# Moving group 1's K and q transposes, one slot of its value products, a split weight cast and paired remainder scores in a fused attention + MLP kernel

## Chip, cores and metric

The kernel runs on one core of a Trainium2 chip. The metric is the device time of one execution in microseconds (us), of which the profile's span is about 1.7 us less.

## The reference, cut to what matters

```python
# q, k, v: (8 blocks, 8 heads, 576 tokens, 64); x: (4608, 512); w_in: (512, 2048); w_out: (2048, 512)
k_p = k.reshape(B, H, 72, 8, D).mean(axis=3)          # K and v pooled by 8 along the sequence
v_p = v.reshape(B, H, 72, 8, D).mean(axis=3)
attn = softmax(q @ k_p.T / sqrt(D))
x = concat_heads(attn @ v_p)
out = gelu_tanh(x @ w_in) @ w_out
```

## The kernel before

The 4608 tokens are worked off in nine groups: 512 tokens of each of the eight blocks, and one remainder group R with the last 64 tokens of every block. While TensorE runs the MLP of one group, the attention of the next is slipped between its matmuls. Python "hooks" say before which matmul (slot) a piece of work is put into TensorE's stream. In group 0, slots 0 to 127 are the hidden product (0.109 us each), 128 to 191 the output product (0.216 us each). Hooks set only the order on each engine; semaphores do the waiting.

Names in the views: kvb is pooled K or v, kbd and vbd are the block-diagonal weights made of them ("spread"), kT and qT are transposes, sc the scores, e their exponentials, r one over the sums of e, eb the softmax weights, eT their transpose, xo the value products, xT their cast, which is the input of the hidden product, gT the hidden product after gelu, osb an output before its store. w_out's "rows 6 and 7" are its blocks 6 and 7 of 128 rows.

```python
def cast_w_out(f0, f1, eng):                 # f32 staging buffer -> bf16 weights
    copy(eng, w_out_b[:, f0:f1, :], w_out_s[f0 // 8][:, f0 - o:f1 - o, :])

def norm(g, j, eng):                         # softmax: two SBUF inputs, e and r
    sums(g, j); nc.vector.reciprocal(out=r, in_=den)
    eng.tensor_tensor(out=o, in0=e, in1=r.to_broadcast(...), op=ALU.mult)

def spread_v(b, eng, parts=(0, 1, 2)):       # pooled v into block-diagonal weights vbd
    ...
# hooks of group 0's MLP, which carry group 1's attention
at(hooks, 72, pool, 1, 0, 4)                 # K pooled on VectorE, c = 4 after it
at(hooks, 80, cast_q, 1, 0, 2, nc.vector)
at(hooks, 108, k_transpose_pe, 1, 0, 5)
at(hooks, 108, k_spread, 1, [nc.vector, nc.vector])     # kT (PSUM) -> kbd
for j in range(4):
    at(hooks, [115, 119, 123, 126][j], q_transpose_pe, 1, j, nc.vector, "sc")
at(hooks, 110, cast_w_out, 0, 1, nc.gpsimd)  # then 1..2, 2..4, 4..6, 6..8 on GpSimd
...
for j in range(4):
    at(hooks, [128, 131, 142, 146][j], scores, 1, j)
    at(hooks, [128, 131, 142, 146][j], exps, 1, j)
    at(hooks, [142, 146, 150, 154][j], norm, 1, j, nc.vector)
    at(hooks, [142, 146, 150, 154][j], e_transpose_dma, 1, j)
for i in range(2):
    at(hooks, 160, pool, 1, 5 + 2 * i, 7 + 2 * i)        # v pooled
    at(hooks, 160, spread_v, 1, nc.gpsimd, (0, 1) if i == 0 else (2,))
tail_of_attention(hooks, 1, 187)             # value products, then xT on ScalarE
```

For later groups the K and q transposes are DMA transposes; R's scores are sixteen 64 x 64 matmuls per j.

The softmax here doesn't subtract the row's maximum and nothing guards it: scores larger than these inputs give would overflow.

## Time and profile before

| | before |
|---|---|
| median of the first three runs | 295.06 us (294.63 to 295.13) |
| span of the profiled run | 293.1 us |
| TensorE busy | 286.0 us, 98% |
| start of group 1's third hidden matmul | 52.78 us |
| end of GpSimd's last w_out cast | 39.87 us |

A line of the timeline has the start in us, the length in us, the engine, the line of the kernel, the operation, output and inputs, the count, and in brackets the idle time before it with what ended it.

### The profile page before, as it was taken

Reading aid. Unit: us, or ns where it says so; the run is one execution under the profiler, and the core shown is the slowest. Engines: PE = TensorE matmul, PEld = TensorE weight load, DVE = VectorE, ACT = ScalarE, POOL = GpSimd, SP = SyncE. Lnnn points to the kernel's source line nnn. Section 1 sums busy time; section 2 is a strip of 40 time slices with the busy share of each in tenths; the row PEclk is TensorE's granted clock in tenths of the full one; section 3 lists DMA queues with packets and bytes.
Section 4 is the critical chain, followed back from the end, with each engine's and each line's share of the span. In section 5 each row is a group of like instructions: output and inputs, shape, how many; then the busy total and the mean of one; then the engine's idle time right before and its main releaser. Section 6 shows DMA issues by size and latency. Waiting matters only on the chain.

```text
span 293.1 us, 4588 instructions
## 1 busy us (share of the span) xinstructions
PE 286.0 (98%) x1739; PEld 143.5 (49%) x1739; DVE 141.0 (48%) x235; ACT 156.5 (53%) x233; POOL 64.3 (22%) x86
## 2 busy tenths in 40 slices
PE   8889899999999999999999999999999999999996
PEld 4678754445444544454445444544444544444444
DVE  5891878176517460747075706580738100920012
ACT  1586484778076706671577256725673377436500
POOL 4575443221303040204002400240024000100000
PEclk9999999999999999999999999999999999999999
DMA  7999999996799369946994599159944900351012
GB/s 231 353 384 345 379 383 208 348 246 165 149 296 279 104 134 287 265 128 134 277 269 148 126 252 298 14 122 247 284 141 103 179 27 2 83 114 38 0 72 72
DMA packets 73301, 56.32 MB, mean 192 GB/s; under 512 B 45888, under 2 KB 55488, under 8 KB 73280
## 3 DMA queue, kind: packets, MB, share of 16 engines
q1 hardware_dynamic: 73136, 55.98, 70.3%
q8 instruction: 13, 0.21, 0.3%
q14 instruction: 8, 0.07, 0.1%
q10 hardware_dynamic: 144, 0.07, 0.1%
HBM read 36.70 MB, written 9.44 MB: 157 GB/s over the span
## 4 chain that ended last, share of the span: by engine, by line
PE 87%; DMA 8%; DVE 1%; SPq 1%; ACT 1%; POOL 0%; issue 0%
PE mm L360 41%; PE mm L344 38%; DMA kv<-in_k_dram 5%; DMA q_sb<-in_q_dram 3%; PE xo L310 3%; PE sc L214 2%; PE mm L388 1%; PE mm L355 1%; SPq L99 1%; ACT xT L79 1%; PE xo L319 1%; DVE kv L132 1%; PE tp L199 0%; POOL q_b L81 0%; PE sc L221 0%; DVE kv L133 0%
## 5 line engine op out<-in xcount | busy, mean ns | idle before, releaser
L360 PE MATMUL mm<-w_out_b,gT 128*128 128x512 bf16 x560 | 128.8, 379 | 0.0
L344 PE MATMUL mm<-xT,w_in_b 128*128 128x512 bf16 x512 | 112.0, 379 | 0.2 <-ACT xT L79 0.2
L346 ACT ACTIVATE gT<-mm 128x512 bf16<-128x512 f32 x128 | 76.4, 597 | 38.4 <-PE mm L344 38.4
L360 PEld LDWEIGHTS <-gT 128*128 128x128 bf16 x560 | 52.8, 98 | 59.7 <-issue 2.9
L344 PEld LDWEIGHTS <-w_in_b 128*128 128x128 bf16 x512 | 50.1, 98 | 60.8 <-issue 0.5
L81 DVE COPY osb<-mm 128x512 f32<-128x512 f32 (+2 forms) x37 | 24.3, 658 | 58.9 <-PE mm L360 52.7
L79 ACT CAST xT<-xo 128x1024 bf16<-128x1024 f32 (+1 forms) x18 | 16.6, 967 | 56.5 <-PE xo L310 48.2
L154 POOL TENSOR_TENSOR vbd<-kvb,vmask 128x256 bf16<-128x256 bf16 (+2 forms) x40 | 21.5, 559 | 104.5 <-DVE kvb L134 104.3
L236 DVE TENSOR_REDUCE den<-e 128x8 f32<-128x576 f32 x36 | 26.5, 736 | 36.9 <-ACT e L229 36.9
L132 DVE TENSOR_TENSOR kv<-kv 128x1024 f32<-128x1024 f32 (+3 forms) x19 | 21.7, 1144 | 38.0 <-DMA kv<-in_v_dram 31.8
L229 ACT ACTIVATE e<-sc 128x576 f32<-128x576 f32 x36 | 22.5, 650 | 9.5 <-ACT e L229 5.6
L248 DVE TENSOR_TENSOR eb<-e,r 128x576 bf16<-128x576 f32 x24 | 22.6, 943 | 1.0 <-DVE r L245 0.2
L81 POOL CAST q_b<-q_sb 128x2048 bf16<-128x2048 f32 (+2 forms) x9 | 17.4, 1937 | 14.2 <-DMA q_sb<-in_q_dram 14.2
L248 POOL TENSOR_TENSOR eb<-e,r 128x576 bf16<-128x576 f32 x6 | 6.9, 1150 | 58.3 <-ACT e L229 31.1
L355 PE MATMUL mm<-xT,w_in_b 128*128 128x256 bf16 x128 | 15.5, 273 | 0.5 <-DVE xT L81 0.5
L214 PE MATMUL sc<-kbd,qT 128*128 128x144 bf16 x128 | 13.3, 226 | 0.3 <-DVE qT L81 0.2
L214 PEld LDWEIGHTS <-qT 128*128 128x128 bf16 x128 | 10.0, 98 | 7.0 <-issue 0.5
L355 PEld LDWEIGHTS <-w_in_b 128*128 128x128 bf16 x128 | 12.1, 98 | 2.1 <-issue 0.6
L357 ACT ACTIVATE gT<-mm 128x512 bf16<-128x512 f32 x16 | 9.4, 597 | 6.5 <-PE mm L355 6.5
L133 DVE TENSOR_TENSOR kv<-kv 128x512 f32<-128x512 f32 (+3 forms) x19 | 12.4, 651 | 0.6
L557 ACT ACT_TABLE_LOAD x8 | 10.3, 1283 | 0.1
L373 ACT ACT_TABLE_LOAD x7 | 9.0, 1283 | 0.1
(62 smaller groups left out, 123.7 us busy)
## 6 DMA issues: line engine op xcount, KB each, us to landing
out_dram<-osb SPq DMA_DIRECT2D x31, 256.0 KB, 7.0
kv<-in_k_dram SPq DMA_DIRECT2D x7, 1024.0 KB, 7.2
q_sb<-in_q_dram SPq DMA_DIRECT2D x7, 1024.0 KB, 6.1
kv<-in_v_dram SPq DMA_DIRECT2D x6, 1024.0 KB, 9.1
w_in_s<-in_moe_w_in_dram SPq DMA_DIRECT2D x8, 512.0 KB, 9.8
w_out_s<-in_moe_w_out_dram SPq DMA_DIRECT2D x4, 1024.0 KB, 13.8
kv<-in_v_dram SPq DMA_DIRECT2D x4, 512.0 KB, 10.2
out_dram<-osb SPq DMA_DIRECT2D x9, 128.0 KB, 2.3
```

The lines of the kernel that those rows point to most:

```text
L79: eng.copy(out=out, in_=in_)
L81: eng.tensor_copy(out=out, in_=in_)
L132: add(out=t[:, :, 0:4, :], in0=t[:, :, 0:4, :], in1=t[:, :, 4:8, :], op=ALU.add)
L154: eng.tensor_tensor(out=vbd[p0:128, b, n0:n1, :].rearrange("p (c r) (hh d) -> p c (r hh) d", c=max(m, 1), d=D), in0=kvb[p0:128, 4 + c0:4 + ...
L214: nc.tensor.matmul(out=o, lhsT=qT[:, j, pr, :], rhs=kbd[:, g, pr].rearrange("d hh s -> d (hh s)"), start=True, stop=True)
L229: nc.scalar.activation(out=e.rearrange("p (x h) s -> p x (h s)", x=2), in_=sc[:, :, 0:4 * Sp], func=ACT.Exp, scale=1.0 / 64.0)
L236: nc.vector.reduce_sum(out=den, in_=e, axis=AX.X)
L248: eng.tensor_tensor(out=o.rearrange("p (h s) -> p h s", s=Sp), in0=e, in1=r.unsqueeze(2).to_broadcast([128, H, Sp]), op=ALU.mult)
L344: nc.tensor.matmul(out=hp, lhsT=w_in_b[:, ko, fo * 128:(fo + 1) * 128], rhs=st[g]["xT"][:, ko, :], start=(i == 0), stop=(i == KO - 1))
L346: nc.scalar.activation(out=gT[:, fo, :], in_=hp, func=ACT.Gelu_apprx_tanh)
L355: nc.tensor.matmul(out=hp[:, f, :], lhsT=w_in_b[:, ko, (fo + f) * 128:(fo + f + 1) * 128], rhs=st[g]["xT"][:, ko, c0:c0 + 256], start=(ko ...
L360: nc.tensor.matmul(out=o, lhsT=gT[:, fo, r * 128:(r + 1) * 128], rhs=w_out_b[:, fo, :], start=(fo == 0), stop=(fo == FO - 1))
```

## The change

The intent: fill the hole that the K transposes leave while pooled K is not there, start the first product without waiting behind a long cast, use the time won for earlier value products, and enter small-tile matmuls two times instead of four in group R.

```diff
-    cast_w_in(0, 2, nc.vector)
+    cast_w_in(0, 2, nc.vector, 0, 256)
     scores(0, 2)
 ...
     scores(0, 3)
+    cast_w_in(0, 2, nc.vector, 256, 512)
     sums(0, 2)
 ...
-    at(hooks, 108, kT_tile, 1, "sc")          # and qT_tile, k_transpose_pe, k_spread
+    at(hooks, 113, kT_tile, 1, "sc")
     for j in range(4):
-        at(hooks, [115, 119, 123, 126][j], q_transpose_pe, 1, j, nc.vector, "sc")
+        at(hooks, [118, 121, 124, 127][j], q_transpose_pe, 1, j, nc.vector, "sc")
 ...
-    tail_of_attention(hooks, 1, 187)
+    tail_of_attention(hooks, 1, 186)
 ...
             for j in range(4):
-                at(hooks, [67, 69, 78, 82][j], scores, n, j)
-                at(hooks, [67, 69, 78, 82][j], exps, n, j)
+                sj = ([67, 67, 80, 80] if n == R else [67, 69, 78, 82])[j]
+                at(hooks, sj, scores, n, j)
+                at(hooks, sj, exps, n, j)
```

More of the change, by code (lines that the diff above doesn't have):

```diff
@@ L573 @@
     at(hooks, 80, cast_q, 1, 2, 4, nc.gpsimd)
-    at(hooks, 108, kT_tile, 1, "sc")
-    at(hooks, 108, qT_tile, 1)
-    at(hooks, 108, k_transpose_pe, 1, 0, 5)
-    at(hooks, 108, k_spread, 1, [nc.vector, nc.vector])
+    at(hooks, 113, kT_tile, 1, "sc")
+    at(hooks, 113, qT_tile, 1)
+    at(hooks, 113, k_transpose_pe, 1, 0, 5)
+    at(hooks, 113, k_spread, 1, [nc.vector, nc.vector])
     for j in range(4):
-        at(hooks, [115, 119, 123, 126][j], q_transpose_pe, 1, j, nc.vector, "sc")
+        at(hooks, [118, 121, 124, 127][j], q_transpose_pe, 1, j, nc.vector, "sc")
     at(hooks, 110, cast_w_out, 0, 1, nc.gpsimd)
```

## The prediction

> **What bounds the kernel now.** I read the page's busy and chain parts first, then TensorE's waits, then the timeline around each place that the diff touches.
>
> ```profile
> PE 286.0 (98%) x1739; PEld 143.5 (49%) x1739; DVE 141.0 (48%) x235; ACT 156.5 (53%) x233; POOL 64.3 (22%) x86
> ...
> PE 87%; DMA 8%; DVE 1%; SPq 1%; ACT 1%; POOL 0%; issue 0%
> ```
>
> TensorE is busy 98% of 293.1 us and carries 87% of the chain that ended last. The diff removes no matrix work, so only holes in TensorE's stream can be won. Its waits:
>
> ```profile
> PE kT L180 <- DVE kvb L147: 0.7, 1, 0.7
> ...
> PE mm L355 <- DVE xT L81: 0.5, 1, 0.5
> ...
> PE mm L344 <- ACT xT L79: 0.2, 1, 0.2
> ```
>
> The first is the K transposes of group 1, the second the start of the first product, the third the start of group 1's product. These are idle times after modelled, overlapping ends. Start to start the holes are larger: the last K transpose starts 0.90 us later than its predecessor's columns explain, the next matmul another 0.10, and group 1's third hidden matmul 0.36 late. From 53 us on no wait remains; the only repeated losses are about 0.096 us where TensorE enters or leaves small-tile matmuls.
>
> The timeline at the K transposes, then at the start of the output product (columns: start us, length us, engine, line, what, releaser):
>
> ```profile
> 31.39 0.40 PE L180 MATMUL kT<-identb,kvb 128*128 128x128 bf16 x4
> ...
> 32.28 0.18 DVE L147 COPY kvb<-kvb 128x64 bf16<-128x64 bf16 x1
> 32.50 0.69 DVE L81 CAST q_b<-q_sb 128x1024 bf16<-128x1024 f32 x1
> ...
> 32.52 0.20 PE L180 MATMUL kT<-identb,kvb 64*128 64x64 bf16 x1 [0.74 <-DVE kvb L147]
> ```
>
> ```profile
> 35.14 2.16 POOL L81 CAST w_out_b<-w_out_s 128x512 bf16<-128x512 f32 x3 [1.04 <-DMA w_out_s<-in_moe_w_out_dram]
> ...
> 35.94 0.60 ACT L357 ACTIVATE gT<-mm 128x512 bf16<-128x512 f32 x1 [0.72 <-PE mm L355]
> 35.99 0.81 PE L360 MATMUL mm<-w_out_b,gT 128*128 128x512 bf16 x3
> ...
> 36.56 1.28 ACT L402 ACT_TABLE_LOAD   x1
> ```
>
> Four K transposes go, then TensorE stands until the pooled last chunk is there at 32.46. That time is set by a load, not by TensorE: VectorE began that chain at 28.66, when block 1's K landed. At 35.14 the same backlog delivers the first output weights; GpSimd's first cast ends at 35.755 (0.617 us each) and TensorE uses it at 35.99, only 0.24 later. Last, the value products of group 1:
>
> ```profile
> 48.99 0.97 POOL L154 TENSOR_TENSOR vbd<-kvb,vmask 128x256 bf16<-128x256 bf16 x2 [0.23 <-DVE kvb L134]
> ...
> 50.02 0.10 PEld L310 LDWEIGHTS <-vbd 32*64 32x64 bf16 x1 [0.25 <-POOL vbd L154]
> ...
> 50.81 1.93 ACT L79 CAST xT<-xo 128x1024 bf16<-128x1024 f32 x2 [4.21 <-PE xo L310]
> ...
> 52.78 13.54 PE L344 MATMUL mm<-xT,w_in_b 128*128 128x512 bf16 x62 [0.20 <-ACT xT L79]
> ```
>
> The last GpSimd spread ends at 49.96 and releases a value matmul at 50.02; the second xT cast, queued behind it on ScalarE, ends at 52.73 and releases the hidden product at 52.78. So group 1 starts when GpSimd's spread allows, not when TensorE reaches its slot.
>
> **The Trainium skill.** "TensorE: Matmul & The Clock Gate", section "Back-to-back issue gap", gives N/2.4 + 2.5 ns for an isolated warm gap: 109 ns for 256 columns, 216 for 512. The trace agrees: 109 and 216 ns start to start. "TensorEngine Tiling (Array Packing)", section "Key Properties", says that changing the tiling mode drains TensorE; the trace shows 0.096 to 0.098 us at each of the eight switches around the remainder's scores. "DMA: Bandwidth & Descriptors", section "Queues, rings and completion order", says descriptors are consumed in ring order; this trace's landings agree, K at 28.64, q at 32.41, w_out at 35.08, 37.78, 40.48 and 43.20, the order of issue. So TensorE's schedule cannot hasten them.
>
> **The change, part by part.**
>
> *K and q transposes later.* Slots 108 to 112, five matmuls of 0.109 us, now fill the hole: TensorE resumes at 32.655 as before, but with slot 113 instead of 108. Gain 0.545 there. The q transposes then need VectorE's cast, which ends 32.50 + 0.69 = 33.19, about 33.25 with 0.055 of semaphore delay, against arrival at 32.655 + 0.56 = 33.21: lose 0.04. PSUM allows the new spacing: kbd copies end 33.73, the second q transposes come at 33.81; each qT copy (0.425) is done before its buffer's next use. The first product's last matmul starts near 35.135 instead of 35.633: 0.50 earlier. The first output matmul, however, cannot start before 35.755 + 0.055 = 35.81 instead of 35.99. **TensorE keeps only 0.18 in the output product.** But last gelu, table load and exponentials hang on the hidden product and do move by 0.50. They lead VectorE's unbroken chain from 38.54 (sums, norms, pooling of v), then GpSimd's spreads. I take 0.05 off for VectorE and GpSimd slowing each other (the same 256-element addition is 0.425 alone and 0.717 beside a spread). v's two parts land at 44.53 and 45.84, before their pooling at 45.0 and 46.4. So the spread ends near 49.51: 0.45 earlier.
>
> *Values one slot sooner.* They would have moved by 0.18 only; with one output matmul (0.216) fewer ahead they come at 49.17, and again wait for the spread until 49.56. The slot is thus needed to use the 0.45, not a gain on top of it. xT follows, and group 1's third hidden matmul starts near 52.33 instead of 52.785. Gain 0.45, carried on.
>
> *Remainder's scores in pairs.* In the chain, with ordinary scores below for comparison:
>
> ```profile
> 216.19 0.25 PE sc L221 x16
> 216.44 0.54 PE mm L360 x2
> ...
> 247.12 0.25 PE sc L214 x4
> 247.37 0.43 PE mm L360 x2
> ```
>
> The 0.11 more on two output matmuls is the entry drain of the next group; the exit drain lies inside the 0.25. Four groups become two: four of eight switches go, 4 x 0.097 = 0.39 us. The third scores need the buffer that the first exponentials leave at about 218.2, and come near 219.4: no wait. No wait follows until the end, so all 0.39 counts.
>
> *Cast of w_in in halves.* xT is no longer behind a 1.17 us cast but a 0.6 one, so the first product's third matmul can start at about 17.65 instead of 17.90, ScalarE's xT becoming the limit. The second half delays VectorE's sums by about 0.19; slots 16, 28 and 32 wait for it. TensorE arrives at the old slot 108 about 0.1 late, not early. Either way it then waits for pooled K until 32.52: room 0.25. Counted as zero.
>
> Sum: 0.45 + 0.39 = 0.84; 295.06 - 0.84 = **294.2 us**.
>
> **Rivals.** *All hidden gains add:* 0.25 at the start, 0.545 at K, 0.22 for the slot, 0.39, giving 293.65. Against it: K's landing absorbs the first and the spread the third. *The w_out wait carries through:* if the q transposes run late, or gelu does not move, only 0.18 to 0.2 remains at group 1: 294.5. For it: slack of only 0.24 at 35.99. Against: gelu does not wait for w_out. *Group 2's K is stuck on the transfers.*
>
> ```profile
> 65.85 0.68 DVE L81 COPY kbd<-kTd 64x288 bf16<-64x288 bf16 x2 [1.67 <-DMA kTd<-kvb]
> ...
> 66.81 0.41 PE L214 MATMUL sc<-kbd,qT 128*128 128x144 bf16 x4
> ```
>
> Copies end at 66.53, slack 0.28 less 0.055. DMA is at 90% or more in that stretch; if it does not move with the rest, TensorE waits 0.2 there and 294.45 results. Against: after the e transposes the engines are nearly idle from 47.8 to 48.3 us, so the next loads start when issued, and that issue follows the norms 0.45 earlier. *Bigger VectorE delay at the start:* if it passes 0.25 us, K is late and up to 0.3 goes.
>
> **Range and chances.** Model errors pull mostly to less gain (0.2 each from two rivals), one to more. The three runs of before spread over 0.5 us, which any median of few runs inherits. I take 293.7 to 294.8. Two per cent is 5.9 us; the holes that the diff touches sum to under 3 us, and no part adds work to TensorE. Within 2%: 0.98.
>
> **What would show it.** In the trace of the changed kernel: the wait of K's last transpose down from 0.74 to about 0.2 us or less; a new wait at the first output matmul on GpSimd's w_out cast, about 0.3; exponentials at 37.35 instead of 37.85; a value matmul still released by the spread, near 49.6; group 1's hidden wait on xT still there; two pairs of 32 remainder matmuls and four switches. I am wrong if the spread no longer gates (more gain), if the scores of group 2 wait for kbd, or if the pairs wait for a PSUM buffer.

## More of the kernel before

The lines that carry the argument stand in the prediction. One pair that it did not read belongs beside them, from the timeline of before:

```profile
37.84 2.03 POOL L81 CAST w_out_b<-w_out_s 128x1024 bf16<-128x1024 f32 x2 [0.54 <-DMA w_out_s<-in_moe_w_out_dram]
...
39.56 0.91 DVE L248 TENSOR_TENSOR eb<-e,r 128x576 bf16<-128x576 f32 x1
```

GpSimd's two casts end at 39.87. VectorE's first norm of group 1 overlaps them and lasts 0.91 us, where group 1's three later norms last 0.76.

## The result, and the profile after

The changed kernel took 294.55 us (median of four, 294.32 to 295.41), the one before 295.10 us in the same rounds. A ratio here is the mean time of one kernel's runs over the mean of the other's runs of the same rounds, so not quite the ratio of the medians. It is 0.999, 95% interval 0.9968 to 1.0013: 0.3 us by the means, 0.55 by the medians, where 0.84 was forecast. The time lies in the range of 293.7 to 294.8, which holds gains from 0.3 to 1.4 us; that it fell there says nothing for the mechanism. Three later sets of rounds gave 0.9987, 1.0004 and 0.9982.

TensorE's busy line and its waits after the change:

```profile
PE 284.2 (97%) x1712; PEld 142.8 (49%) x1739; DVE 141.8 (48%) x236; ACT 156.4 (53%) x233; POOL 64.7 (22%) x86
```

```profile
PE mm L360 <- issue: 0.8, 5, 0.2
...
PE mm L355 <- DVE xT L81: 0.2, 1, 0.2
...
PE kT L180 <- DVE kvb L147: 0.2, 1, 0.2
```

K's wait fell from 0.7 to 0.2 as intended. The 27 matmuls fewer are records that this trace lacks (1712 matmuls for 1739 weight loads); the five "issue" waits in the first line, 0.16 us each, are seeming holes of this kind: each stands where the record of the first matmul behind a block of small ones is missing. The timeline at the start of the output product and up to group 1's product:

```profile
35.04 2.16 POOL L81 CAST w_out_b<-w_out_s 128x512 bf16<-128x512 f32 x3 [1.05 <-DMA w_out_s<-in_moe_w_out_dram]
...
35.71 0.81 PE L360 MATMUL mm<-w_out_b,gT 128*128 128x512 bf16 x3
...
35.96 1.28 ACT L402 ACT_TABLE_LOAD   x1
```

```profile
37.73 2.03 POOL L81 CAST w_out_b<-w_out_s 128x1024 bf16<-128x1024 f32 x2 [0.53 <-DMA w_out_s<-in_moe_w_out_dram]
...
38.96 1.41 DVE L248 TENSOR_TENSOR eb<-e,r 128x576 bf16<-128x576 f32 x1
...
40.29 0.74 DVE L236 TENSOR_REDUCE den<-e 128x8 f32<-128x576 f32 x1
```

```profile
49.91 0.10 PEld L310 LDWEIGHTS <-vbd 32*64 32x64 bf16 x1 [0.24 <-POOL vbd L154]
...
50.70 1.93 ACT L79 CAST xT<-xo 128x1024 bf16<-128x1024 f32 x2 [4.29 <-PE xo L310]
...
52.68 0.31 PEld L344 LDWEIGHTS <-w_in_b 128*128 128x128 bf16 x2 [0.26 <-issue]
```

ScalarE's table load came 0.60 us earlier (36.56 to 35.96), and the first norm did start 0.60 us earlier. But it now lasts 1.41 us instead of 0.91 and ends only 0.10 earlier; the last value matmul released by the spread, xT and group 1's third hidden matmul are each 0.11 earlier. In this execution the load behind GpSimd's casts was itself 0.10 us earlier (it landed at 37.68 instead of 37.78), so nothing remains of that part.

Group R, in the chain that ended last:

```profile
216.20 0.39 PE sc L221 x32
216.58 0.16 issue
216.74 2.75 PE mm L360 x12
```

One block of 32 score matmuls stands where two of 16 did. From R's first score to its first value matmul before took 13.00 us, after 12.54: 0.46 won. The span is made up so: 0.11 won at group 1's start, 0.06 lost at the scores of group 2 and 0.06 at those of block 4, 0.46 won in R, together 0.45 by the end of the last matmul (290.21 to 289.76).

### The profile page after: what moved, and what is told of

Same layout as the page of the kernel before. It is cut to its first block, busy times and chain, and to the rows that moved or that the text cites. A ratio compares the mean times of both kernels' runs of the same rounds, so it can differ in the third digit from the quotient of the medians. Undisturbed runs are those within 1.5% of the kernel's fastest.

```text
span 292.6 us, 4562 instructions
## 1 busy us (share of the span) xinstructions
PE 284.2 (97%) x1712; PEld 142.8 (49%) x1739; DVE 141.8 (48%) x236; ACT 156.4 (53%) x233; POOL 64.7 (22%) x86
## 4 chain that ended last, share of the span: by engine, by line
PE 81%; DMA 8%; DVE 4%; SPq 3%; ACT 1%; issue 1%; POOL 0%; ACTq 0%
PE mm L360 37%; PE mm L344 36%; DMA w_out_s<-in_moe_w_out_dram 5%; DMA w_in_s<-in_moe_w_in_dram 3%; PE xo L310 3%; PE sc L214 2%; SPq L437 2%; DVE eb L248 1%; ACT gT L346 1%; PE mm L388 1%; DVE den L236 1%; SPq L99 1%; PE xo L319 1%; DVE kv L132 0%; DVE kv L133 0%
## 5 line engine op out<-in xcount | busy, mean ns | idle before, releaser
L360 PE MATMUL mm<-w_out_b,gT 128*128 128x512 bf16 x543 | 125.9, 379 | 1.4 <-issue 0.8
L248 DVE TENSOR_TENSOR eb<-e,r 128x576 bf16<-128x576 f32 x24 | 23.3, 972 | 0.8
L81 POOL CAST w_in_b<-w_in_s 128x512 bf16<-128x512 f32 (+1 forms) x10 | 8.6, 874 | 2.4 <-DMA w_in_s<-in_moe_w_in_dram 2.4
```

What stands on the lines that cost most here:

```text
L81: eng.tensor_copy(out=out, in_=in_)
L248: eng.tensor_tensor(out=o.rearrange("p (h s) -> p h s", s=Sp), in0=e, in1=r.unsqueeze(2).to_broadcast([128, H, Sp]), op=ALU.mult)
L360: nc.tensor.matmul(out=o, lhsT=gT[:, fo, r * 128:(r + 1) * 128], rhs=w_out_b[:, fo, :], start=(fo == 0), stop=(fo == FO - 1))
```

## The experiments

**The theory (port).** VectorE's norm reads two SBUF inputs, and GpSimd's cast reads SBUF. While GpSimd holds the port that the two share, the norm does not run, and the profile counts its waiting as busy time. So the norm ends a fixed time after the cast of w_out rows 6 and 7, and that cast is set by a load. Behind the norm, three more norms, the pooling of v, the spread, the last value products and xT follow one on another up to group 1's third hidden matmul. **Rivals:** the norm is slower for another reason; the value slot matters; the start-up cast matters; group 2's K is the gate. Times below are read from single instructions in each trace; "cast" is GpSimd's last cast of w_out before group 1's spreads, "third hidden" is group 1's third hidden matmul.

### The change again, the pairs alone, and the change without the pairs

The pairs alone are the last hunk of the diff on the kernel before; the third kernel is the change without that hunk. One chip, five rounds.

> The changed kernel itself, for the same chip and rounds as the others. New theory (port): VectorE's first norm of group 1 ends 0.61 us after GpSimd's cast of w_out rows 6 and 7, in every kernel that leaves that cast where it is, because it reads two SBUF inputs and GpSimd holds the port; that cast is set by a load. Then only the paired scores gain: 0.4 us against before, ratio 0.9986. Theory of the prediction: 0.84 us, ratio 0.997.

> The kernel before with the paired remainder scores and nothing else. Port theory: this alone is the whole gain, 0.39 us, ratio 0.9987; group 1's third hidden matmul starts where it does in before (52.7 to 52.8 us). Prediction: also 0.39 us, which would leave it 0.45 us slower than the changed kernel; by the port theory it is within 0.1 us of it.

> The change without the paired scores. Port theory: no gain against before beyond the load's own jitter of 0.1 us, ratio 1.000; the first norm of group 1 starts about 0.6 us earlier than in before but lasts 1.4 us instead of 0.9. Prediction: 0.45 us faster than before, ratio 0.9985.

Measured: the change 0.9987 (0.9974 to 1.0), median 294.69; the pairs alone 0.9984 (0.9971 to 0.9997), median 294.53; without pairs 0.9999 (0.9987 to 1.0011), median 295.15; before 295.11. The pairs alone gain as much as the whole change. All other parts together give nothing that these rounds can see; their interval just excludes the 0.9985 that the prediction asks of them. One of the six runs with the pairs alone took 295.71, so outliers of over 1 us need no other part of the change.

| trace | cast ends | norm starts | norm lasts | norm end - cast end | third hidden - cast end |
|---|---|---|---|---|---|
| before | 39.87 | 39.56 | 0.91 | 0.61 | 12.92 |
| the change | 39.76 | 38.96 | 1.41 | 0.61 | 12.91 |
| pairs alone | 39.97 | 39.76 | 0.82 | 0.61 | 12.92 |
| without pairs | 39.98 | 39.21 | 1.37 | 0.61 | 12.91 |
| K and q back | 39.85 | 39.57 | 0.89 | 0.61 | 12.91 |
| cast twice | 41.06 | 40.41 | 1.25 | 0.60 | 12.91 |

The norm may start 0.9 us or 0.2 us before the cast's end; it ends 0.6 us after it. If the two shared bandwidth, a norm that starts earlier would end earlier. Group 1's start follows 12.9 us after the cast, whatever the hooks are. The eight other traces that leave the cast on GpSimd give the same 0.61 and 12.91 to 12.92.

### The last cast issued twice

```diff
     at(hooks, 110, cast_w_out, 6, 8, nc.gpsimd)
+    at(hooks, 110, cast_w_out, 6, 8, nc.gpsimd)
```

> The change with GpSimd's cast of w_out rows 6 and 7 issued twice, the same result. Port theory (the whole instruction is excluded): the first norm still starts near 38.96 us and its end moves by one whole cast, about 0.99 us, to 0.61 us after the second cast's end: it lasts about 2.4 us. If VectorE and GpSimd shared the bandwidth instead, it would lengthen by at most a few tenths. Group 1's third hidden matmul then starts about 1 us later than in the changed kernel, near 53.6.

```profile
37.92 3.13 POOL L81 CAST w_out_b<-w_out_s 128x1024 bf16<-128x1024 f32 x3 [0.68 <-DMA w_out_s<-in_moe_w_out_dram]
...
40.41 1.25 DVE L248 TENSOR_TENSOR eb<-e,r 128x576 bf16<-128x576 f32 x1
```

The norm's end moved with the second cast, to 0.60 us after it, and the third hidden matmul to 53.97, 12.91 us after the cast. The expected start of 38.96 was missed: in this execution TensorE came to the K transposes at 33.60 instead of 31.90, for a reason that the half cast below explains, and the norm started at 40.41. So its length is not the 2.4 us that was expected, and the run does not test a wait of that length; its end is where the port theory puts it.

### The port freed

```diff
-    at(hooks, 110, cast_w_out, 6, 8, nc.gpsimd)
+    at(hooks, 110, spread_v, 1, nc.gpsimd, (-1,))   # new part of spread_v: its first multiplication, before the casts
 ...
         at(hooks, [128, 131, 142, 146][j], exps, 1, j)
+        if j == 1:
+            at(hooks, 131, cast_w_out, 6, 8, nc.scalar)
```

> The change with the cast of w_out rows 6 and 7 moved from GpSimd to ScalarE behind the second exponentials, and GpSimd's first spread done before its casts, so that GpSimd holds no port while the first norm runs. Port theory: that norm lasts about 0.76 us instead of 1.41 and ends near 39.75; the last spread ends near 48.8 instead of 49.46; group 1's third hidden matmul starts near 52.1 instead of 52.68; 0.4 to 0.6 us faster than the changed kernel. If the norm is slow for another reason (its first use of the sums, PSUM, ScalarE's table load), it stays near 1.4 us and the time does not move.

```profile
38.21 1.04 POOL L81 CAST w_out_b<-w_out_s 128x1024 bf16<-128x1024 f32 x1 [0.52 <-DMA w_out_s<-in_moe_w_out_dram]
...
39.45 0.76 DVE L251 TENSOR_TENSOR eb<-e,r 128x576 bf16<-128x576 f32 x1
```

The norm is at 0.76 us: GpSimd's work beside it was the reason. (A trace shows only that one waits for the other; that what they share is a port is no trace's word.) Counted from the start of GpSimd's cast of rows 4 and 5 (which follows the same load; it was 0.48 us later in this execution, and that load was issued before the first edited instruction), the third hidden matmul comes after 14.34 us instead of 14.94: **0.60 us won**. But the time did not follow: 0.9985 (0.9973 to 0.9997), as the change. Group 2's scores in the same trace:

```profile
66.30 0.64 DVE L81 COPY kbd<-kTd 64x288 bf16<-64x288 bf16 x2 [1.71 <-DMA kTd<-kvb]
...
67.08 0.41 PE L217 MATMUL sc<-kbd,qT 128*128 128x144 bf16 x4 [0.35 <-DVE kbd L81]
```

They follow the third hidden matmul by 14.53 us instead of 14.03. Of the 0.60 won, 0.50 is lost in this trace to K of group 2, which hangs on a DMA transpose. This is the third rival of the prediction, come one step later. It takes small amounts of the change as well: 0.06 us in the first trace, 0.28 in the one without pairs, none in three others.

### Slot, start-up cast, K and q undone one at a time

Each is the change with one hunk of the diff reversed; one look each, read from the traces.

> The change with the value products of group 1 back at the old slot. Port theory: as the spread gates them, it matters little: the last small value matmul still starts 0.05 us after the spread's end, and group 1's third hidden matmul starts where it does in the changed kernel, within 0.1 us. If the slot matters, that matmul is 0.2 us later.

> The change with the w_in cast in one piece again. Prediction's step and port theory alike: the wait for pooled K absorbs it; TensorE resumes after the K transposes 0.17 us after VectorE's copy ends in both, and everything behind is unmoved within 0.1 us. Rival: the earlier start of the first product is worth up to 0.25 us.

> The change with the K and q transposes back at their old slots. Port theory: the hole at the K transposes is back at 0.7 us and the exponentials come 0.6 us later than in the changed kernel, but the first norm still ends 0.61 us after GpSimd's cast, so group 1 starts within 0.1 us of the changed kernel. Prediction: group 1 starts 0.45 us later.

Third hidden minus cast end: 12.92, 12.91 and 12.91 us. None of the three parts moves group 1's start. With the value products back at their old slot, they start at 49.57 and the third hidden matmul still waits for the same spread. With the w_in cast whole, TensorE still waits 0.23 us for K's last chunk. With K and q back, the norm starts 0.6 us later, at 39.57, and ends as ever after the cast.

### Block 2's v load moved behind group 2's transposes

```diff
     # load_kv: k, half k, half v as before, then
-            load_main(b, "v", 0, 4, nc.sync)
+            if n != 2:
+                load_main(b, "v", 0, 4, nc.sync)
 ...
+                    at(hooks, t0 + 1, load_main, b, "v", 0, 4, nc.sync)   # group 1's MLP, and
+                # v's pooling and spread at slots 57 and 58 instead of t0 + 20 and t0 + 21
```

> The port-free kernel, and block 2's main v load issued behind group 2's q and K transposes instead of before them, its pooling behind the kbd copies. Theory (second gate): in the port-free kernel group 1 started 0.60 us earlier measured from the load that feeds GpSimd's last casts, but group 2's scores waited for K, which hangs on the transfers. Freed of it, kbd copies end about 2.4 us earlier, the scores of group 2 follow group 1's third hidden matmul by 14.03 us as in before, and the kernel is about 1.0 us faster than before (ratio 0.9965) and 0.55 us faster than the change. Rival (nothing but jitter): ratio 0.9985 as the change.

> The change with only that v load moved. Port theory: group 1 still starts 14.94 us after the cast's load is used; the wait of group 2's scores (0.06 us in the changed kernel's trace, 0.28 in the one without pairs) goes, so 0 to 0.3 us faster than the change, ratio to before 0.998. If group 2's K were the real gate of the change, it would gain the whole 0.45.

> The changed kernel again, for the same chip and rounds: ratio to before 0.9987 as in the earlier five rounds; group 1's third hidden matmul 14.94 us after GpSimd's cast of w_out rows 4 and 5 starts.

Both are slower: 1.0066 (1.0042 to 1.0091) and 1.0047 (1.0016 to 1.0077), with the change at 1.0004 (0.9986 to 1.0022). Counted from the cast of rows 4 and 5, the kbd copies did end 1.9 and 2.4 us earlier, and group 2's scores came 14.03 us after the third hidden matmul. But the load now stood before group 2's e transposes, and the value products waited. In the trace of the change with v later:

```profile
81.39 1.18 PE L310 MATMUL xo<-eT,vbd 32*64 32x512 bf16 x16 [1.60 <-DMA eT<-eb]
```

A wait was moved, not removed. The edit was bad; the reading of group 2's gate stands. (The trace of the port-free version also lost the race of the half cast, below: its third hidden matmul comes 15.58 us after the cast of rows 4 and 5 starts instead of 14.34, and that is not the v load's doing.)

### Group 0's stores moved instead, with and without the freed port

In both kernels the w_in cast is whole again. The four stores of group 0's output (256 KB each) are held back and issued behind group 2's K transpose; what stands in the queue before the e transposes stays the same in sum.

```diff
         copy(eng, osb, o)
-        store(g, r, osb)
+        if g == 0: held.append((r, osb))
+        else: store(g, r, osb)
 ...
                 at(hooks, t0, k_transpose_dma, b)
+                if n_ == 1: at(hooks, t0, store_held)
```

> Paired scores, K and q later, values one slot sooner, w_in cast whole, the last w_out cast on ScalarE (port free), and group 0's four stores issued behind group 2's q and K transposes. Theory: group 1's third hidden matmul 14.34 us after GpSimd's cast of w_out rows 4 and 5 starts; kbd copies of group 2 about 2.4 us earlier, its first scores 14.03 us after that hidden matmul, no new wait, as the queue's sum before the e transposes is the same. 1.06 us faster than before: ratio 0.9964. Rival (something else binds): 0.9985.

> The change with the w_in cast whole and group 0's stores behind group 2's transposes, but the port not freed. Port theory: group 1 still starts 14.94 us after the cast; group 2's scores no longer wait, 14.03 us after the third hidden matmul. 0.46 us faster than before, ratio 0.9984. If group 2's K were the main gate, it would be as fast as the kernel with both.

> The change with the w_in cast whole. Without the race its executions lie close together: ratio 0.9984 to 0.9990 and none over 1 us above the fastest.

> The change again. Race theory: most executions as with the whole cast, some 0.7 to 1.3 us slower, so that its mean is 0.1 to 0.4 us above that of the whole cast: ratio 0.9985 to 1.0. If the halves cost nothing, the two agree within 0.1 us.

| kernel | median | ratio to before | 95% interval |
|---|---|---|---|
| before | 295.08 | 1 | |
| the change | 294.49 | 0.9982 | 0.9969 to 0.9995 |
| the change, w_in cast whole | 294.67 | 0.9985 | 0.9971 to 0.9998 |
| and stores later | 294.55 | 0.9985 | 0.9973 to 0.9998 |
| and port free | 293.98 | **0.9965** | 0.9953 to 0.9978 |

The version with both is 1.0 us faster than before by the means, where 1.06 was expected. Four of its five executions (293.79 to 294.03) are shorter than all fifteen of the other three changed kernels (294.14 and more). In its trace the third hidden matmul comes 14.39 us after the cast of rows 4 and 5 starts, and the scores of group 2 follow it by 14.03:

```profile
38.56 1.04 POOL L81 CAST w_out_b<-w_out_s 128x1024 bf16<-128x1024 f32 x1 [0.47 <-DMA w_out_s<-in_moe_w_out_dram]
...
39.79 0.76 DVE L251 TENSOR_TENSOR eb<-e,r 128x576 bf16<-128x576 f32 x1
```

```profile
65.50 0.55 DVE L81 COPY kbd<-kTd 64x288 bf16<-64x288 bf16 x1
...
66.98 0.41 PE L217 MATMUL sc<-kbd,qT 128*128 128x144 bf16 x4
```

kbd is there 0.9 us early. It came 1.2 us earlier than in the port-free kernel, counted from the same cast, and not the 2.4 that were expected. The trace as a whole is no shorter than that of the stores alone (292.8 and 292.7 us): it is of the slowest of the five executions, and its cast of rows 4 and 5 starts 0.66 us later (38.56 against 37.90). Moving the stores without freeing the port gives nothing over the whole cast (294.55 and 294.67, both 0.9985); in its trace the third hidden matmul comes 14.94 us after the cast and the scores of group 2 14.03 after it, as expected. Each gate had to go for the other's removal to count.

**The half cast.** The timeline of the change at start-up, then of the kernel with the cast issued twice:

```profile
17.30 1.32 POOL L81 CAST w_in_b<-w_in_s 128x1024 bf16<-128x1024 f32 x1 [0.80 <-DMA w_in_s<-in_moe_w_in_dram]
17.30 0.41 DVE L81 CAST w_in_b<-w_in_s 128x512 bf16<-128x512 f32 x1
```

```profile
17.30 1.04 POOL L81 CAST w_in_b<-w_in_s 128x1024 bf16<-128x1024 f32 x1 [0.77 <-DMA w_in_s<-in_moe_w_in_dram]
17.33 1.29 DVE L81 CAST w_in_b<-w_in_s 128x512 bf16<-128x512 f32 x1
```

The second half starts within 30 ns of a GpSimd cast, and one of the two engines waits for the other. In nine of the eleven traces with halves VectorE won (GpSimd's record starts at most 23 ns before it) and its cast took 0.41 us. In two, GpSimd started 28 and 30 ns ahead, VectorE took 1.29, TensorE waited 0.99 and 0.59 us (0.98 and 0.70) for two of group 0's norms, where the change's trace waits at most 0.12, and reached the last K transpose near 34 us instead of 32.4 to 33. The second of the two is the port-free kernel with v later. But the timed rounds show no cost: the change 0.9982, with the whole cast 0.9985; the executions of the whole cast only lie closer together (294.49 to 294.74 against 294.14 to 295.04). Whether the two slow runs of the third set (296.09 and 296.26) lost this race is not known, as they left no trace.

## Why the prediction was right or wrong, point by point

- **Pairs of remainder scores: right.** 0.39 forecast, 0.46 measured. Start to start, a block of 16 costs 0.093 us on entry, 0.105 on exit, 0.02 more before its second four matmuls than before the later ones, and 0.011 at the matmul behind it, 0.23 in all; the forecast had the first two. Why the other two arise is not shown. It is the whole gain that the rounds show.
- **The hole at K and the w_out wait: right.** The wait fell to 0.2 us; TensorE starts the output product at 35.71 after a wait of 0.31 for GpSimd's cast (0.3 was written; counted start to start, the cast ends at 35.66); table load and exponentials moved by 0.60 (0.50 was written; q's load, on which the q transposes hang, landed 0.10 earlier in this execution).
- **The step that failed** is the one that says "I take 0.05 off for VectorE and GpSimd slowing each other", and with it "So the spread ends near 49.51: 0.45 earlier". The term measured 0.50: the norm grew from 0.91 to 1.41 us. The spread ended at 49.85, 0.11 earlier, all of it the load's. I had treated the port as a tax on speed, and reckoned with "VectorE's unbroken chain from 38.54"; it is broken at the first norm by a wait that shows as a longer instruction. "SBUF — State Buffer" of the Trainium skill, section "SBUF: two separate sides", says that the shared pair is "an exclusive lock, not a bandwidth split" and that the later of a GpSimd instruction and a VectorE one with two SBUF inputs waits for the whole instruction. The runs agree: the constant 0.6 us after the cast, the second cast, and 0.76 us with the port free. The prediction does not use this page. It had a second case in hand, the addition that takes 0.425 us alone and 0.717 beside a spread, and read it as slowing; in the traces of before, the change and the port-free kernel it ends 0.28 to 0.29 us after that spread's end, so it fits a wait.
- **Values one slot sooner: right in kind.** The spread still gates; the slot alone is worth nothing, and the time that it was to use did not come. Whether the slot is needed once that time is won was not tested.
- **The halves counted as zero: right on the clock,** for the reason given (K's load absorbs it), and the first product's third matmul started at 17.65 as written. But the first half took 0.87 us beside a GpSimd cast, not 0.6, TensorE came to the K transposes 0.03 us early and not 0.1 late, and the close race of the second half with GpSimd was missed.
- **The rival "group 2's K is stuck on the transfers"** was real. It took 0 to 0.28 us of the change from trace to trace, and 0.50 of what the freed port won. The prediction argued that the next loads would be issued earlier with the norms. In the port-free kernel the norms were 0.65 us earlier, but the queue issued the q load as late as before (9.08 us after the cast of rows 4 and 5 starts, 9.12 before), so that argument failed too. The time is lost in the issue of group 1's third e transpose: it took 1.70 us before and 2.30 with the port free, and ended 7.75 and 7.71 us after that cast starts, in both 0.24 to 0.25 us before the last part of block 1's v landed. Where it started later (cast twice) it took 1.20. That fits an issue that is held by the loads ahead of it in the queue; the reason is not shown.

## What to carry to other kernels

Before counting on a chain to move, look for an instruction in it that is longer than its twins, and ask whether its end stands at a fixed distance from another engine's; that is a wait that no list of waits shows. VectorE work with two SBUF inputs, or a cast from SBUF to SBUF such as the one of 0.41 us here, should not be planned beside GpSimd work whose start a load decides. When one gate is taken away, check the next one in the same trace: here freeing the port alone and unblocking the queue alone each gave nothing that the rounds could see, and both together a further 0.5 to 0.6 us.

## What the Trainium skill lacked or had wrong

- "SBUF — State Buffer", "SBUF: two separate sides": right about the lock, but it does not say how the lock looks in a profile. Here the blocked time is counted as busy, in either engine: a norm of 0.76 us shows as 1.41, a VectorE cast of 0.41 us as 1.29, a GpSimd cast of 1.04 us as 1.32, and no wait is listed.
- "TensorEngine Tiling (Array Packing)", "Key Properties": right that a mode switch drains, without a figure. Here the first 64 x 64 matmul starts 0.309 us after a 512-column one, where 0.216 is usual: 0.093 for the switch (the prediction wrote 0.096 to 0.098). In all 0.23 us is saved for each pair of 64 x 64 blocks that is joined.
- "TensorE: Matmul & The Clock Gate", "Back-to-back issue gap": its isolated gap (216 ns for 512 columns) is what this kernel shows in sustained streams with a weight load for every matmul; its sustained figure of 131 ns does not appear here.
- No page that I read gives the time for which the issue of one DMA transpose of these sizes holds the SP queue on this chip: group 2's q transposes held it for 5.66 us in the kernel before, later ones for 1.33 to 2.00 us, and group 1's transposes of eb for 1.20 to 1.70, in the port-free kernel for up to 2.30.
